# Moving ScalarE's copies of x ahead of its other copies, and GpSimd's last rows into the expert stage, in a sketch-attention and hash-routing kernel on one Trainium2 core

## The chip, the cores and the metric

One core of one Trainium2 chip runs the kernel. The metric is the device time of one execution in microseconds (us). The kernel before takes 200.77 us, the median of 3 runs (200.69 to 201.09). The profiled execution took 200.42 us and its records span 198.7 us. All times inside the profile are counted from the start of that span.

The engines are TensorE (PE in the profile; PEld is its loading of weights), VectorE (DVE), ScalarE (ACT), GpSimd (POOL) and SyncE (SP, which here only starts transfers).

## What is computed

Two blocks follow each other. The first is an attention without softmax: q and k are turned into 64 features each by products of two 8-wide sketches, keys and values are summed into one 64 x 32 matrix per head, and each query reads that matrix and divides by a normaliser. The second block sends each of the 4352 rows to one of 8 experts, chosen by a hash of its token number, and applies two layers with a ReLU between.

```python
# batch 4, heads 4, seq 1088, head_dim 32, r 8; experts 8, width 128, hidden 1024
def phi(x):
    a = einsum('rd,bhsd->bhsr', S1, x)
    b = einsum('rd,bhsd->bhsr', S2, x)
    return einsum('bhsi,bhsj->bhsij', a, b).reshape(..., r * r)
kv  = einsum('bhsf,bhsd->bhfd', phi(k), v);  z = phi(k).sum(over s)
x   = einsum('bhsf,bhfd->bhsd', phi(q), kv) / (einsum('bhsf,bhf->bhs', phi(q), z) + 1e-6)
x   = x.transpose(0, 2, 1, 3).reshape(4352, 128)
e   = token_ids * 2654435761 % 8
out[rows of e] = relu(x[rows of e] @ w1[e]) @ w2[e]
```

## The kernel before

The kernel fixes the order of the instructions on each engine itself: within one engine they run as the program text emits them. So the place of a copy in the text is its place in the engine's queue.

Each batch has 1088 positions: 1024 "main" ones in two groups of 512 (`g = 0, 1`), and a "tail" of 64. The attention of one batch makes these steps. TensorE multiplies features of k by v (`kv_products`), ScalarE spreads the result over block-diagonal matrices `m` in 16 small copies (`kv_diagonal`) and two for the tail (`kv_tail`), and TensorE multiplies the features of q by `m` (`x_products`, two tiles in a group, each followed by a copy from PSUM by ScalarE).

```python
ps   = tile_pool(name="ps", bufs=4, space=PSUM)     # k, q products, transposes, hp
ps_x = tile_pool(name="ps_x", bufs=2, space=PSUM)   # x products
ps_o = tile_pool(name="ps_o", bufs=2, space=PSUM)

def x_products(b, g, fT, m, psum=x_bank):           # x_bank: a tile of ps_x
    for h0 in range(0, H, 2):                       # two tiles in a group
        p = psum([P, 2, Q * DA], "x_ps")
        for h in range(2):
            for fb in range(FB):
                nc.tensor.matmul(p[:, h], fT[...], m[fb][...], ...)
        nc.scalar.copy(xes[b % 2][...], p[:])       # line 617

def transposed(src, g):                             # 4 transposes of k, then ScalarE's copy
    p = bank([P, H, P], "kT_ps")
    ...
    nc.scalar.copy(kT[:], p[:])                     # line 426
```

`copied(ab_ps)` copies the sketch products of k or of q from PSUM (two copies, line 467), `route_tiles_p()` is one scaling pass of ScalarE over a routing table (line 393), and `q_tail_copied` copies the tail's products of q. The loop over the first two batches (`EB` is 2) is where they meet:

```python
for b in range(EB):
    kv = kv_products(b, ...)
    if b > 0: abk_ps = k_products(kTs)
    abq_ps = q_products(qT, T)
    va = values(v_t[b + 1], T, work, "")
    ...
    m = kv_diagonal(b, kv)
    if b > 0:
        abk = copied(abk_ps)
        route_tiles_p()
    if b == 0:
        tail = q_tail_copied(abt_ps)
    abq = copied(abq_ps)
    m_tail = kv_tail(b, kv)
    if b == 0:
        kTs = [transposed(k_t[b + 2], g) for g in range(0, T, Q)]
    kp = k_features(abk, T, work, "")               # VectorE
    ...
    for g in range(GQ):
        x_products(b, g, fTs[g], m)
    x_tail_products(b, m_tail)
    qT = q_blocks(q_t[b + 2], T)
    if b == 0: ... route_rows(0); route_tiles()     # VectorE
    else:
        kTs = [transposed(k_t[b + 2], g) for g in range(0, T, Q)]
        route_rows(1)
    denominators(b, ...)                            # VectorE
    for g in range(GQ): x_main(b, g, nc.gpsimd)     # rows of x, then their transfer to memory
    x_tail(b, nc.gpsimd)
    ...
```

The last two batches follow outside the loop. The rows of x go to a scratch tensor in memory (`x_rows`). The expert stage gathers them by index, 128 rows at a time, with an indirect transfer that GpSimd starts (`fetch_tile`), turns them on their side (`turn_in`, a transfer; `join_in`, VectorE), and multiplies. The first 16 gathered tiles take rows of batches 0 and 1 alone; only the later ones, of the second round over the experts, read rows of batches 2 and 3.

```python
denominators(e, 0, GQ * HQ + H)                     # e: the last batch
for g in range(GQ):
    x_main(e, g, nc.gpsimd)
x_tail(e, nc.gpsimd)
...
def at(g, c, f, *a): ...                            # f is emitted beside step c of expert group g
ahead = [(k, j) for k in range(3, 11) for j in range(tiles_of(k)[1])]
for g, n in enumerate((2, 4, 2, 2, 2, 2, 2, 2)):
    for c in range(n): at(g, 1 + c, fetch_tile, *ahead.pop(0))
for k in range(2, G):
    at(k - 1, 0, turn_in, k)
    at(k - 1, 5, join_in, k)
for g in range(G - 1):                              # 16 groups of 8 steps
    for c in range(FC):
        layer1(g, c)                                # 2 matmul records, then hT by ACT or DVE
        if g > 0: layer2(g - 1, c)                  # 2 matmul records
        for f in beside.get((g, c), ()): f()
```

Each `fetch_tile` of these first copies its indices on VectorE into one of four small buffers, so that VectorE waits in its queue for the gather of four tiles earlier.

Of the kernel before, what the change touches and what calls it, by code (L numbers as in the profile page):

```python
# [30 lines left out]
def kernel(  # L31
# [12 lines left out]
    nc = tc.nc  # L44
    P = 128
    B, H, S, D = q.shape
# [4 lines left out]
    T = S // P  # L51
    SM = T * P
    SP = S - SM
    TT = B // 2
    Q = P // D
# [28 lines left out]
    def bank(shape, name):  # L84
        return ps.tile(shape, F32, tag="b", name=name)
# [13 lines left out]
    def tail_rows(b):  # L99
        return slice(b // TT * SP, (b // TT + 1) * SP)  # L100

    def load_tail_part(t, src, b, eng):
        eng.dma_start(t[tail_rows(b)].rearrange("p t h d -> p (t h) d"),
                      src[b:b + TT, :, SM:, :].rearrange("t h p d -> p (t h) d"))

    def load_tail(src, name, n=B):

        t = const.tile([P, TT, H, D], F32, name=name)
        for b in range(0, n, TT):
            load_tail_part(t, src, b, nc.sync)  # L110
        return t

    def load_main(src, b, tag):
# [11 lines left out]
    k_t, v_t, q_t = [], [], []  # L125
# [23 lines left out]
    k_tail = load_tail(k, "k_tail")  # L149
    v_tail = load_tail(v, "v_tail")  # L150
    q_t.append(load_main(q, 1, "q"))
    q_tail = load_tail(q, "q_tail", TT)
    v_t.append(load_main(v, 1, "v"))
    for b in range(2, B):
        load_batch(b)
# [53 lines left out]
    GQ = T // Q  # L209
# [12 lines left out]
    hi, lo = s64[:, :, 1], s64[:, :, 0]  # L222
# [169 lines left out]
    def route_tiles_p():  # L392
        nc.scalar.activation(tiles[:, :, 0], in_tile[:], AF.Copy, scale=p1[:])
# [23 lines left out]

    x_dram = nc.dram_tensor("x_rows", (N, DM), F32)

    def transposed(src, g):  # L420

        p = bank([P, H, P], "kT_ps")
        for h in range(H):
            nc.tensor.transpose(p[:, h], src[:, h, g:g + Q].rearrange("p t d -> p (t d)"), ident[:])
        kT = work.tile([P, H, P], F32, tag="kT", name="kT", bufs=2)
        nc.scalar.copy(kT[:], p[:])
        return kT
# [35 lines left out]
    def ab_tile():  # L463
        return work.tile([P, T, H, 2, R], F32, tag="ab", name="ab", bufs=3)
# [5 lines left out]
    def copied(ab_ps):  # L470

        ab = ab_tile()
        for g in range(0, T, Q):
            copy_ab(ab, ab_ps, g)
        return ab
# [59 lines left out]
    def kv_tail(b, kv):  # L535

        m = m_tails[b % 2]
        for h in range(2):
            r = slice(h * R * R, (h + 1) * R * R)
            nc.scalar.copy(m[r, :, h], kv[r, :, h * DA:(h + 1) * DA])  # L540
        return m
# [15 lines left out]
    def q_features(ab, g):  # L557

        f = work.tile([P, Q, H, FB * D], F32, tag="f", name="f", bufs=1)
        features(f[:].rearrange("p q h (i j) -> p (q h) i j", i=R), ab[:, g * Q:(g + 1) * Q].rearrange("p q h x r -> p (q h) x r"))  # L560
        fT = feats.tile([P, H * FB, P], F32, tag="fT", name="fT", bufs=3)
        nc.vector.transpose(fT[:].rearrange("p k (q s) -> p k q s", q=Q), f[:].rearrange("p q h (k d) -> p (h k) q d", d=D))  # L562
        return fT
# [44 lines left out]
    def x_products(b, g, fT, m, psum=x_bank):  # L608

        for h0 in range(0, H, 2):  # L610
# [3 lines that stand above are left out]
                    nc.tensor.matmul(p[:, h], fT[:, (h0 + h) * FB + fb],  # L614
                                     m[fb][:, h0 + h].rearrange("p t d -> p (t d)"),
                                     start=(fb == 0), stop=(fb == FB - 1), skip_group_check=True)
            nc.scalar.copy(xes[b % 2][:, (g * H + h0) * Q:(g * H + h0 + 2) * Q].rearrange("p (h t) d -> p h (t d)", h=2), p[:])  # L617
# [12 lines left out]
    dens, rows_of = {}, {}  # L630
# [5 lines left out]
        nc.vector.tensor_scalar(den, xes[b % 2][:, lo:hi, D], 1e-6, None, op0=OP.add)  # L636
        nc.vector.reciprocal(den, den)  # L637

    def x_main(b, g, eng):
        if g == 0:  # L640
            rows_of[b] = work.tile([P, T, H, D], F32, tag="xs", name="xs", bufs=1)
        eng.tensor_tensor(rows_of[b][:, g * Q:(g + 1) * Q].rearrange("p t h d -> p h t d"),  # L642
                          xes[b % 2][:, g * HQ:(g + 1) * HQ, 0:D].rearrange("p (h t) d -> p h t d", h=H),
                          dens[b][:, g * HQ:(g + 1) * HQ].rearrange("p (h t) -> p h t", h=H).unsqueeze(3)
                          .to_broadcast([P, H, Q, D]), op=OP.mult)
        n = parts(b)
        if n > 1 or g == GQ - 1:
            ts = slice(g * Q, (g + 1) * Q) if n > 1 else slice(0, T)
            lo = b * S + ts.start * P
            nc.sync.dma_start(x_dram[lo:lo + SM // n].rearrange("(p t) d -> p t d", t=T // n),  # L650
                              rows_of[b][:, ts].rearrange("p t h d -> p t (h d)"))

    def x_tail(b, eng):
        rows = tail_rows(b)
        xs_tail = work.tile([P, H, D], F32, tag="xs_tail", name="xs_tail", bufs=1)
        eng.tensor_tensor(xs_tail[rows], xes[b % 2][rows, GQ * HQ:, 0:D],
                          dens[b][rows, GQ * HQ:].unsqueeze(2).to_broadcast([SP, H, D]), op=OP.mult)
        nc.sync.dma_start(x_dram[b * S + SM:(b + 1) * S], xs_tail[rows].rearrange("p h d -> p (h d)"))


    route_experts()
    kTs = [transposed(k_t[0], 0)]
# [3 lines left out]
    route_scan()  # L666
    va = values(v_t[0], T, work, "", None)
    route_firsts()
    load_tail_part(q_tail, q, TT, nc.gpsimd)
    abk = ab_tile()  # L670
    kp = work.tile([P, T, H, R, R], F32, tag="kp", name="kp", bufs=1)
    parts_ps = [k_products(kTs[g:g + 1]) for g in range(GQ)]
# [5 lines left out]
    for g in range(GQ):  # L678
        ts = slice(g * Q, (g + 1) * Q)
        nc.scalar.copy(va[:, ts, :, 0:D], v_t[0][:, :, ts].rearrange("p h t d -> p t h d"))  # L680
    kTs = [transposed(k_t[1], g) for g in range(0, T, Q)]
    kv = kv_products(0, (kp, va), (kp_tail, va_tails), None, upto=Q)
# [6 lines left out]
    abq = ab_tile()  # L689
# [5 lines left out]
    for u, va_tail in enumerate(va_tails):  # L695
        rows = tail_rows(u * TT)
        nc.gpsimd.tensor_copy(va_tail[rows, :, :, 0:D], v_tail[rows])
    kv = kv_products(0, (kp, va), (kp_tail, va_tails), kv, Q + 2)
    route_digits(digits)
    abt = k_tail_products(kTt)  # L700
    abk_ps = k_products(kTs)
    kv = kv_products(0, (kp, va), (kp_tail, va_tails), kv, T)
    abk = copied(abk_ps)
    fTs = [q_features(abq, 0)]
# [5 lines left out]
    for b in range(EB):  # L710
        kv = kv_products(b, (kp, va), (kp_tail, va_tails), None if b else kv)
        if b > 0:
            abk_ps = k_products(kTs)
# [3 lines that stand above are left out]
            route_slots()  # L717
        if b == 0:
            abt_ps = q_tail_products(qT_tail)
        m = kv_diagonal(b, kv)  # L720
        if b > 0:
            abk = copied(abk_ps)
            route_tiles_p()
        if b == 0:
            tail = q_tail_copied(abt_ps)
        abq = copied(abq_ps)
        m_tail = kv_tail(b, kv)
        if b == 0:
            kTs = [transposed(k_t[b + 2], g) for g in range(0, T, Q)]
        kp = k_features(abk, T, work, "")  # L730
        if b == 0:
            fT_tail = q_tail_features(tail)
        for g in range(GQ):
            x_products(b, g, fTs[g], m)
        x_tail_products(b, m_tail)
        qT = q_blocks(q_t[b + 2], T)
        if b == 0:
            fTs = [q_features(abq, 0)]
            route_rows(0)
            route_tiles()  # L740
        else:
            kTs = [transposed(k_t[b + 2], g) for g in range(0, T, Q)]
            route_rows(1)
        denominators(b, 0, GQ * HQ + H)
        for g in range(GQ):
            x_main(b, g, nc.gpsimd)
        x_tail(b, nc.gpsimd)
        if b == 0:
            load_experts(range(E // 2, E - 2))
        if b == 0:  # L750
            fTs.append(q_features(abq, 1))
        else:
            fTs = [q_features(abq, 0)]
# [83 lines left out]
    b, e = EB, EB + 1  # L837
    kv = kv_products(b, (kp, va), (kp_tail, va_tails))
    idx = route_list()
    abk_ps = k_products(kTs)  # L840
    abq_ps = q_products(qT, T)
    va = values(v_t[e], T, work, "")
    fTs.append(q_features(abq, 1))
    m = kv_diagonal(b, kv)
    abk, abq = copied(abk_ps), copied(abq_ps)
    m_tail = kv_tail(b, kv)
# [7 lines left out]
    kv = kv_products(e, (kp, va), (kp_tail, va_tails))  # L854
# [5 lines left out]
    m_tail = kv_tail(e, kv)  # L860
    load_experts([E - 1], nc.scalar)
    fTs = [fT, q_features(abq, 1)]
# [8 lines left out]
    x_products(e, 1, fTs[1], last_m)  # L871
    x_tail_products(e, m_tail)
    denominators(e, 0, GQ * HQ + H)
    for g in range(GQ):
        x_main(e, g, nc.gpsimd)
    x_tail(e, nc.gpsimd)

    feats.release()
    hots.release()
# [125 lines left out]
    def at(g, c, f, *a):  # L1005
        beside.setdefault((g, c), []).append(lambda: f(*a))
# [8 lines left out]
    for g, n in enumerate((2, 4, 2, 2, 2, 2, 2, 2)):  # L1015
        for c in range(n):
            at(g, 1 + c, fetch_tile, *ahead.pop(0))
    assert not ahead
    for k in range(11, G):
        for j in range(tiles_of(k)[1]):  # L1020
            at(k - 3, 1 + j, fetch_tile, k, j)
# [28 lines left out]
    g, lo = G - 1, GL - P  # L1050
# [40 lines left out]
    with tc.For_i(0, turns):  # L1091
# [19 lines left out]
        at = moe.tile([P, C], F32, tag="at", name="at", bufs=1)  # L1111
# [3 lines left out]
        rows = moe.tile([P, C, P], BF16, tag="hT", name="rows", bufs=2)  # L1115
# [66 lines left out]
```

## Time and profile before

| Engine | busy us | share of the span |
|---|---|---|
| PE | 187.1 | 94% |
| PEld | 156.0 | 79% |
| DVE | 108.2 | 54% |
| POOL | 104.9 | 53% |
| ACT | 73.5 | 37% |

The shares are averages over two stages of different nature. From the start to about 65 us (the attention and the routing) all engines take turns; from 65 us to about 190 us (the experts) TensorE runs nearly alone. A share for the whole span does not say what a change in one of them brings. What is to be read is where TensorE stands idle, since everything at the end hangs on its last product.

In the timelines each line has the start in us, the busy time in us of the merged instructions, the engine, the line of the kernel, the operation, what it writes and reads, and how many instructions were merged. A bracket at the end gives the idle time of that engine ahead of the instruction and what ended it. The busy times of TensorE's records overlap each other a little, so starts are compared with starts.

### The profile page before, as it was taken

To read this page: it belongs to the slowest core of one execution; us is meant where nothing else is said; L and a number is where in the kernel's file an instruction comes from. 1 tells how busy PE (TensorE), PEld (TensorE's weight loads), DVE (VectorE), ACT (ScalarE), POOL (GpSimd) and SP (SyncE) were. 2 spreads that over 40 slices of the span, in tenths; PEclk is the share of its full clock that TensorE was granted. 3 is DMA by queue.
4 is the path that set the end of the run, shared out by engine and by line. 5 is a ranking of instruction groups with operands and counts; after the bars stand their busy time and mean duration, and the time that the engine had idled before them with its cause. 6 is when DMAs were issued, how large, how long until landed. Compare 5 with 4: busy or idle time off the path is not lost. (4 is left out here: it accounts for less than half of the span.)

```text
span 198.7 us, 3355 instructions
## 1 busy us (share of the span) xinstructions
PE 187.1 (94%) x1066; PEld 156.0 (79%) x1066; DVE 108.2 (54%) x299; ACT 73.5 (37%) x227; POOL 104.9 (53%) x141
## 2 busy tenths in 40 slices
PE   8999969799999999999999999999999999999970
PEld 3889969799998888788888887777777777677960
DVE  5699999589659634434443553544537454332320
ACT  6543953944637412323323332313323131322120
POOL 7328963327642677276468466556365540534541
PEclk9999999999999999999999999999999999999995
DMA  4999999995186453143143244234251331410100
GB/s 135 298 189 296 352 353 337 348 361 190 26 241 196 154 165 92 43 92 79 41 107 84 54 91 105 56 78 69 52 113 42 92 75 33 78 26 25 47 23 14
DMA packets 40242, 26.10 MB, mean 131 GB/s; under 512 B 21273, under 2 KB 37404, under 8 KB 40224
## 3 DMA queue, kind: packets, MB, share of 16 engines
q1 hardware_dynamic: 35360, 19.08, 35.3%
q0 software_dynamic: 2336, 4.66, 8.9%
q10 hardware_dynamic: 2528, 2.13, 3.6%
q8 instruction: 9, 0.15, 0.3%
q14 instruction: 9, 0.07, 0.1%
HBM read 17.47 MB, written 4.59 MB: 111 GB/s over the span
## 5 line engine op out<-in xcount | busy, mean ns | idle before, releaser
L892 PE MATMUL hp<-xT,w 128*128 128x256 f32 (+3 forms) x272 | 81.9, 394 | 0.4 <-DVE hT L765 0.4
L900 PE MATMUL op<-hT,w 128*128 128x256 f32 (+2 forms) x256 | 79.0, 399 | 0.0
L765 DVE TENSOR_SCALAR hT<-hp 128x256 f32<-128x256 f32 (+3 forms) x68 | 29.7, 439 | 64.6 <-PE hp L892 39.7
L903 POOL DMA_INDIRECT out_dram<-os,put x36 | 36.3, 1010 | 45.7 <-DVE os L956 31.1
L892 PEld LDWEIGHTS hp<-xT,w 128*128 128x128 f32 x272 | 49.7, 190 | 12.9 <-issue 1.0
L900 PEld LDWEIGHTS op<-hT,w 128*128 128x128 f32 x256 | 48.1, 190 | 12.9
L763 ACT ACTIVATE hT<-hp 128x256 f32<-128x256 f32 (+3 forms) x68 | 27.0, 400 | 68.1 <-PE hp L892 51.1
L757 POOL DMA_INDIRECT xg<-x_rows,idx x34 | 35.3, 1038 | 19.6 <-issue 6.7
L614 PE MATMUL x_ps<-m,fT 128*128 128x132 f32 x128 | 16.2, 280 | 3.0 <-ACT xe L617 3.0
L614 PEld LDWEIGHTS x_ps<-m,fT 128*128 128x128 f32 x128 | 15.0, 190 | 3.7 <-ACT xe L617 3.6
L510 PE MATMUL kv<-va,kp 128*128 128x132 f32 x128 | 15.6, 278 | 0.1
L510 PEld LDWEIGHTS kv<-va,kp 128*128 128x128 f32 x128 | 14.9, 190 | 0.4 <-issue 0.3
L642 POOL TENSOR_TENSOR xs<-xe,den 128x512 f32<-128x512 f32 x6 | 7.3, 1229 | 12.3 <-DVE den L637 10.9
L935 ACT COPY half<-op 128x256 uint16<-128x256 uint16 (+1 forms) x26 | 8.8, 392 | 12.8 <-PE op L900 11.9
L532 ACT COPY m<-kv 32x66 f32<-32x66 f32 x48 | 9.9, 206 | 8.7 <-PE kv L510 8.1
L479 DVE TENSOR_TENSOR kp<-ab 128x1024 f32<-128x1024 f32 x8 | 9.5, 1224 | 4.8 <-ACT ab L467 4.8
L562 DVE STREAM_TRANSPOSE fT<-f 128x1024 f32<-128x1024 f32 x8 | 10.0, 1245 | 0.5
L479 DVE TENSOR_TENSOR f<-ab 128x1024 f32<-128x1024 f32 x8 | 10.0, 1251 | 0.1
L834 DVE COPY xT<-xh_turned 128x256 uint16<-128x256 uint16 (+1 forms) x28 | 8.1, 342 | 0.0
L452 PE MATMUL abq_ps<-s_k,qT 128*128 128x128 f32 (+1 forms) x64 | 7.8, 274 | 0.4 <-DVE qT L687 0.4
L828 DVE COPY xh<-xg 128x256 uint16<-128x256 uint16 (+1 forms) x28 | 7.9, 324 | 0.0
L452 PEld LDWEIGHTS abq_ps<-s_k,qT 128*128 128x128 f32 x64 | 7.5, 192 | 0.5 <-issue 0.5
(172 smaller groups left out, 154.1 us busy)
## 6 DMA issues: line engine op xcount, KB each, us to landing
w<-in_moe_w_dram SPq DMA_DIRECT2D x12, 512.0 KB
w<-in_moe_w_dram ACTq DMA_DIRECT2D x4, 512.0 KB
k<-in_k_dram SPq DMA_DIRECT2D x3, 512.0 KB
q<-in_q_dram SPq DMA_DIRECT2D x3, 512.0 KB
v<-in_v_dram SPq DMA_DIRECT2D x3, 512.0 KB
x_rows<-xs SPq DMA_DIRECT2D x3, 512.0 KB
out_dram<-os,put POOLq DMA_INDIRECT x36
xg<-x_rows,idx POOLq DMA_INDIRECT x34
```

The costliest lines, as they stand in the source:

```text
L452: nc.tensor.matmul(dst, stationary, s.rearrange("p t x r -> p t (x r)").unsqueeze(1).to_broadcast([s.shape[0], n, s.shape[1], 2 * R]), sta ...
L479: eng.tensor_tensor(dst, ab[:, :, 0].unsqueeze(3).to_broadcast(shape), ab[:, :, 1].unsqueeze(2).to_broadcast(shape), op=OP.mult)
L510: nc.tensor.matmul(kv[:].rearrange("p x y -> p (x y)")[:, pr * HA:(pr + 1) * HA], kp[:, t, 2 * pr:2 * pr + 2].rearrange("p h i j -> p (h i ...
L532: copy(m[f][t * D:(t + 1) * D, h::2, t], src)
L562: nc.vector.transpose(fT[:].rearrange("p k (q s) -> p k q s", q=Q), f[:].rearrange("p q h (k d) -> p (h k) q d", d=D))
L614: nc.tensor.matmul(p[:, h], fT[:, (h0 + h) * FB + fb], m[fb][:, h0 + h].rearrange("p t d -> p (t d)"), start=(fb == 0), stop=(fb == FB - 1 ...
L757: nc.gpsimd.indirect_dma_start(out=dst, out_offset=None, in_=x_dram[0:rows], in_offset=bass.IndirectOffsetOnAxis(ap=idx, axis=0), bounds_c ...
L763: nc.scalar.activation(dst, src, AF.Relu if relu else AF.Copy)
L765: return nc.vector.tensor_scalar(dst, src, 0.0, None, op0=OP.max).ins
L892: nc.tensor.matmul(hp[:, 0:hi - lo], w1[:, g % E, c * P:(c + 1) * P], x_columns(first_of(g) + lo, first_of(g) + hi), start=True, stop=True)
L900: nc.tensor.matmul(ops[g][:, 0:hi - lo], w2[:, g % E, c], hTs[g][:, c, lo:hi], start=(c == 0), stop=(c == FC - 1))
L903: st_ = nc.gpsimd.indirect_dma_start(out=out[:], out_offset=bass.IndirectOffsetOnAxis(ap=idx, axis=0), in_=src, in_offset=None, bounds_che ...
```

## The change

It has three parts. In the loop over the first two batches, ScalarE's copies are put in another order: the two copies of x of group 0 come ahead of the copies of q's products; the copies of the transposed k (batch 0) and the scaling pass of the routing table (batch 1) come behind all copies of x. TensorE's order stays as it was: for batch 0 the transposes of k are still emitted ahead of the x products, only their copies are later. Second, the rows of the last batch are computed by GpSimd beside steps 6 and 7 of expert group 1 instead of ahead of the expert stage, and their two transfers are started by GpSimd instead of SyncE. Third, the second half of the tail of q is loaded by SyncE, right behind the first half, instead of by GpSimd.

The first part is for the two banks of x products in PSUM, which TensorE can only write again once ScalarE has emptied them. The second lets GpSimd start the gathers of the expert stage before it turns to rows that are needed later.

```diff
-    q_tail = load_tail(q, "q_tail", TT)
+    q_tail = load_tail(q, "q_tail")
@@
-    def transposed(src, g):
+    def turned(src, g):
         p = bank([P, H, P], "kT_ps")
         for h in range(H):
             nc.tensor.transpose(p[:, h], ...)
+        return p
+    def transposed(src, g):
+        return kT_copied(turned(src, g))
+    def kT_copied(p):
         kT = work.tile([P, H, P], F32, tag="kT", name="kT", bufs=2)
         nc.scalar.copy(kT[:], p[:])
         return kT
@@   x_main and x_tail take the queue of their transfer (dma=nc.sync)
@@
-    load_tail_part(q_tail, q, TT, nc.gpsimd)
@@
         m = kv_diagonal(b, kv)
-        if b > 0:
-            abk = copied(abk_ps)
-            route_tiles_p()
         if b == 0:
             tail = q_tail_copied(abt_ps)
-        abq = copied(abq_ps)
-        m_tail = kv_tail(b, kv)
-        if b == 0:
-            kTs = [transposed(k_t[b + 2], g) for g in range(0, T, Q)]
+            kT_ps = [turned(k_t[b + 2], g) for g in range(0, T, Q)]
+        else:
+            abk = copied(abk_ps)
         kp = k_features(abk, T, work, "")
         if b == 0:
             fT_tail = q_tail_features(tail)
-        for g in range(GQ):
-            x_products(b, g, fTs[g], m)
+        x_products(b, 0, fTs[0], m)
+        abq = copied(abq_ps)
+        m_tail = kv_tail(b, kv)
+        x_products(b, 1, fTs[1], m)
         x_tail_products(b, m_tail)
         qT = q_blocks(q_t[b + 2], T)
         if b == 0:
+            kTs = [kT_copied(p) for p in kT_ps]
             fTs = [q_features(abq, 0)]
             ...
         else:
+            route_tiles_p()
             kTs = [transposed(k_t[b + 2], g) for g in range(0, T, Q)]
@@
     denominators(e, 0, GQ * HQ + H)
-    for g in range(GQ):
-        x_main(e, g, nc.gpsimd)
-    x_tail(e, nc.gpsimd)
@@
+    for g in range(GQ):
+        at(1, 6, x_main, e, g, nc.gpsimd, nc.gpsimd)
+    at(1, 7, x_tail, e, nc.gpsimd, nc.gpsimd)
```

More of the change, by code (lines that the diff above doesn't have):

```diff
@@ L100, in tail_rows, with load_tail @@
         return slice(b // TT * SP, (b // TT + 1) * SP)
[L102 to L106, printed above, removed]
+    def load_tail(src, name):
         t = const.tile([P, TT, H, D], F32, name=name)
-        for b in range(0, n, TT):
-            load_tail_part(t, src, b, nc.sync)
+        for b in range(0, B, TT):
+            nc.sync.dma_start(t[tail_rows(b)].rearrange("p t h d -> p (t h) d"),
+                              src[b:b + TT, :, SM:, :].rearrange("t h p d -> p (t h) d"))
         return t
@@ L637, in denominators, with x_main @@
         nc.vector.reciprocal(den, den)
-    def x_main(b, g, eng):
+    def x_main(b, g, eng, dma=nc.sync):
         if g == 0:
@@ L649, in x_main, with x_tail @@
             lo = b * S + ts.start * P
-            nc.sync.dma_start(x_dram[lo:lo + SM // n].rearrange("(p t) d -> p t d", t=T // n),
-                              rows_of[b][:, ts].rearrange("p t h d -> p t (h d)"))
-    def x_tail(b, eng):
+            dma.dma_start(x_dram[lo:lo + SM // n].rearrange("(p t) d -> p t d", t=T // n),
+                          rows_of[b][:, ts].rearrange("p t h d -> p t (h d)"))
+    def x_tail(b, eng, dma=nc.sync):
         rows = tail_rows(b)
@@ L657, in x_tail @@
                           dens[b][rows, GQ * HQ:].unsqueeze(2).to_broadcast([SP, H, D]), op=OP.mult)
-        nc.sync.dma_start(x_dram[b * S + SM:(b + 1) * S], xs_tail[rows].rearrange("p h d -> p (h d)"))
+        dma.dma_start(x_dram[b * S + SM:(b + 1) * S], xs_tail[rows].rearrange("p h d -> p (h d)"))
     route_experts()
```

## The prediction, made before the changed kernel was run

> **What bounds the kernel now.** I read the page's busy shares first: TensorE 94%, the others 37 to 54%. Then the table of stages, to see where the missing 6% are. TensorE's idle time is 6.6 us after 190 us (the last rows leaving), and before that only 0.96 us in 0 to 10, 0.49 in 10 to 20, 0.29 in 20 to 25, 1.38 in 25 to 30, 1.33 in 35 to 40, 0.13 in 60 to 80, 0.37 in 80 to 85 and 0.39 in 180 to 190. Everything else is TensorE at work, so a change that leaves its work alone can win these gaps and no more. Then the timeline of TensorE, to see who ends the two large ones:
>
> ```profile
> 22.75 1.97 PE L614 MATMUL x_ps<-m,fT 128*128 128x132 f32 x16
> 26.38 2.07 PE L614 MATMUL x_ps<-m,fT 128*128 128x132 f32 x16 [1.67 <-ACT xe L617]
> ...
> 36.43 2.02 PE L614 MATMUL x_ps<-m,fT 128*128 128x132 f32 x16
> 39.78 2.07 PE L614 MATMUL x_ps<-m,fT 128*128 128x132 f32 x16 [1.33 <-ACT xe L617]
> ```
>
> Each line of 16 is one group of x, two tiles. The reader sees the second group stand behind a ScalarE copy of x, 1.67 us in batch 0 and 1.33 us in batch 1. ScalarE's timeline says why:
>
> ```profile
> 19.44 3.49 ACT L532 COPY m<-kv 32x66 f32<-32x66 f32 x16 [0.76 <-PE kv L510]
> 22.96 0.85 ACT L590 COPY ab_tail<-abq_ps 32x64 f32<-32x64 f32 x4
> 23.82 0.27 ACT L591 COPY ab_tail<-abq_ps 128x128 f32<-128x128 f32 x1
> 23.98 0.66 ACT L467 COPY ab<-abq_ps 128x256 f32<-128x256 f32 x2
> 24.51 0.44 ACT L540 COPY m_tail<-kv 64x66 f32<-64x66 f32 x2
> 24.97 1.07 ACT L426 COPY kT<-kT_ps 128x512 f32<-128x512 f32 x2
> 25.93 0.68 ACT L617 COPY xe<-x_ps 128x264 f32<-128x264 f32 x2
> ...
> 36.63 0.65 ACT L467 COPY ab<-ab_ps 128x256 f32<-128x256 f32 x2
> 37.16 1.33 ACT L393 ACTIVATE tiles<-in_tile,p 128x1224 bf16<-128x1224 bf16 x1
> 38.38 0.64 ACT L467 COPY ab<-abq_ps 128x256 f32<-128x256 f32 x2
> 38.89 0.43 ACT L540 COPY m_tail<-kv 64x66 f32<-64x66 f32 x2
> 39.35 0.66 ACT L617 COPY xe<-x_ps 128x264 f32<-128x264 f32 x2
> ```
>
> The first x tile of batch 0 is ready about 1 us after 22.75, but its copy starts at 25.93, because three other sets of copies are in the queue before it. In batch 1 the first tile is ready at about 37.4 and its copy starts at 39.35. There are two banks for x, both full, so TensorE stops. ScalarE is not overloaded (37% busy); its order is wrong.
>
> In the expert stage I compared the starts of TensorE's pairs, 0.43 us apart when nothing waits. Two places are off: from 75.23 to 75.84 (0.18 us lost) and from 81.63 to 82.59 (0.53 lost, 0.10 in the pair before). For the first, the timelines of VectorE and of GpSimd:
>
> ```profile
> 73.29 0.15 DVE L809 COPY idx<-get 128x1 int32<-128x1 int32 x1 [0.90 <-DMA xg<-x_rows,idx]
> 74.66 0.15 DVE L809 COPY idx<-get 128x1 int32<-128x1 int32 x1 [1.21 <-DMA xg<-x_rows,idx]
> ```
>
> ```profile
> 67.56 2.05 POOL L642 TENSOR_TENSOR xs<-xe,den 128x512 f32<-128x512 f32 x2 [1.38 <-DVE hT L765]
> 69.69 0.53 POOL L656 TENSOR_TENSOR xs_tail<-xe,den 64x128 f32<-64x128 f32 x1
> 70.49 1.04 POOL L757 DMA_INDIRECT xg<-x_rows,idx  x1 [0.27 <-POOL xs_tail L656]
> ```
>
> Here VectorE stands 0.90 and 1.21 us behind gathers, and GpSimd started these late because it made the last batch's rows first (67.56 to 70.2). VectorE's join of the next input columns (75.06) is late by that, and TensorE's 75.84 waits for it.
>
> **What the Trainium skill says.** "PSUM — Partial Sum Buffer", The four PSUM rules: a matmul's output lies in one bank, and PSUM is TensorE's only way out. So a tile of 264 floats takes a bank and must be copied before the bank is used again; the trace agrees with the 1.67 us above. Its Specifications say that GpSimd reaches no PSUM, so it could not take over copies of x. "ScalarE: Activation LUTs", What ACT_TABLE_LOAD costs, gives an ACTIVATE 186 ns plus 0.833 ns per element, and 93 ns more for a pointer operand. Estimates from it: 406 ns for 264 elements, 1.30 us for the scaling pass of 1224. The trace has 380 ns and 1.33 us; I use those. "SBUF — State Buffer", SBUF: two separate sides: GpSimd and VectorE can lock each other out of a shared port when VectorE reads two SBUF inputs. Moving GpSimd's rows into the experts could meet that; but VectorE's evictions there read PSUM, and they took 0.42 us beside the rows (67.35 to 70.2) as elsewhere. "DMA: Bandwidth & Descriptors", Issuing engines are not separate DMA queues: all transfers share 16 engines whoever starts them, so the two changed queues move no bytes faster. No run shows that apart yet.
>
> **Batch 0.** No instruction is added on ScalarE, TensorE or VectorE; the sum of work stays. ScalarE is free at 24.09 (end of the 0.27). The first x tile, 8 of 16 matmuls in 1.97 us, is ready at about 23.75, so its copy runs 24.1 to 24.5. TensorE finishes the second tile at about 24.7 and finds the first bank free. The second copy runs to 25.15, before the next bank is asked for (about 25.6). The gap of 1.67 closes. Then q's products (0.66), the tail matrix (0.44) and the first copy of group 1 end at about 26.65; the tail product wants that bank at 26.6, a wait of at most 0.1. The batch's x ends near 27.1 instead of 28.76: **1.6 us won**. The k copies (1.07) follow, done at 28.5; TensorE needs them after the next kv product (3.87 + 0.61), at 31.3. VectorE wants q's copies at 26.6 and has them at 25.8.
>
> **Batch 1.** TensorE comes to x at 34.8, m is complete at about 35.0 (all shifted by 1.6, the same touch as before). Copies of k's products to 35.65, first x copy to 36.3, second after its tile (36.7) to 37.1; group 1 starts at 36.7 without a gap. q's copies and the tail matrix end at 38.25, the next x copy at 38.6, the tail product wants its bank at 38.65. So 1.33 more, and the sum of both batches is about **3.0 us**, the 1.67 + 1.33 of the rows above. The scaling pass (1.33) now ends near 40.7 and the k copies near 41.8; TensorE wants the first with the routing product at 47.15 - 3.0 = 44.1 and the second at 45.2. VectorE gets k's copy 1.6 us earlier (it waited 2.31 us for it at 37.03), ends kp at 37.7 and so is ahead of the kv product that now starts at 40.1. GpSimd's rows of batch 1 move up with it, if their buffer is free of the transfer of batch 0; I put that at about 41.
>
> **Batches 2 and 3** keep their order; each step there waits for a product of TensorE or a copy of it, so it moves up by 3.0 as a block. Gathers start at about 48 instead of 50.55 and are wanted at 59.
>
> **Experts.** GpSimd starts the gathers of chunk 3 at about 63.6, where before shifted by 3.0 it would be 67.5. Both VectorE waits (0.90, 1.21) go and with them TensorE's 0.18. The rows (2.05 + 0.53) and two started transfers (an estimate of 1 us each, from the 0.95 us that the tail's load took on GpSimd) then lie at about 72.5 to 77, ahead of gathers that are wanted two groups later (14 us), and the rows themselves are read only from group 4 on, near 90. The loss at 81.63 is not explained: ScalarE and VectorE both stood still with products ready. It may go or stay; I count 0.15 of its 0.63.
>
> **q's tail.** One transfer of 64 KB goes from GpSimd (0.95 us of its queue at 6.24, where it waits for data till 12.99 anyway) to SyncE, 0.6 us there. VectorE reads it at 18.4. I count zero.
>
> **The sum:** 1.6 + 1.4 + 0.18 + 0.15 = 3.3 us. 200.77 - 3.3 = 197.5; I say **197.4 us**.
>
> **Rivals.** (1) *A new wait takes the place of the old:* VectorE is without a gap from 25 to 34.7 and does not move up in batch 0, so TensorE running ahead could meet VectorE's features of q for group 1 (ready 34.72, wanted at 36.7) or row table (ready 40.2, wanted 44.1). The slack is 2 us, so I doubt it; it would leave 1.7 of 3.0 us, about 199. (2) *The gain is given back at the experts* by weights or gathers not there yet: the transfers run full until 46 us, and only GpSimd's gathers could be late; they have 10 us. About 200 if so. (3) *GpSimd's rows in group 1 hold back gathers or evictions*: 0.5 us or so lost, about 198. (4) *The unexplained standstill goes altogether*: 196.9.
>
> **Range and chances.** The 3.0 is read from two gaps and has nothing to hide behind, since TensorE is in one chain from there to the end. The rest is 0 to 0.8 us up, or 0.5 to 1 us down. Range 196.5 to 198.6. Faster by over 2% needs less than 196.75, a win of 4.0 us: 0.12. Within 2%: 0.87. Slower: 0.01.
>
> **What would show it.** TensorE's timeline after: second groups of x at 24.7 and 36.7 without a bracket of over 0.2 us; the first pair of the experts at about 62 instead of 64.97; no wait of VectorE's index copies in group 1; the span near 195.4. I am wrong if the brackets are gone but the first expert pair comes later than 62.5 (rival 1), or comes at 62 and the span is above 196 (rivals 2, 3).

## The result and the profile after

The changed kernel takes 197.79 us, the median of 4 runs (197.51 to 197.99), against 200.88 us of the kernel before (4 runs beside it, 200.69 to 201.09). The ratio is 0.9845, with a 95% interval of 0.9828 to 0.9862: 1.5% less. The span of the profile went from 198.7 to 196.2 us. The engines' busy times and shares of the changed kernel, from its page:

```profile
PE 186.0 (95%) x1066; PEld 155.8 (79%) x1066; DVE 112.2 (57%) x299; ACT 74.0 (38%) x227; POOL 105.5 (54%) x142
```

The counts of instructions are those of before but for the one transfer more that GpSimd starts (two of the rows, one of q's tail less), yet VectorE is busy 4.0 us longer (108.2 before). Nothing was added to VectorE, so something made its instructions longer. That is the second half of this story.

The timeline of TensorE in the changed kernel: the x products of batches 0 and 1, the way into the experts, and one place in the experts.

```profile
22.39 3.77 PE L617 MATMUL x_ps<-m,fT 128*128 128x132 f32 x32
26.09 0.45 PE L626 MATMUL x_ps<-m_tail,fT_tail 128*64 128x66 f32 x4
...
34.14 3.82 PE L617 MATMUL x_ps<-m,fT 128*128 128x132 f32 x32
37.90 0.45 PE L626 MATMUL x_ps<-m_tail,fT_tail 128*64 128x66 f32 x4
...
58.39 0.44 PE L823 MATMUL xp<-ident,xg 128*128 128x128 f32 x2 [0.18 <-ACT xe L620]
59.08 2.04 PE L617 MATMUL x_ps<-m,fT 128*128 128x132 f32 x16 [0.25 <-DVE den L639]
...
61.42 1.99 PE L892 MATMUL hp<-xT,w 128*128 128x256 f32 x8
...
78.58 0.59 PE L900 MATMUL op<-hT,w 128*128 128x256 f32 x2
80.15 0.67 PE L892 MATMUL hp<-xT,w 128*128 128x256 f32 x2 [0.98 <-ACT half L935]
80.66 0.59 PE L900 MATMUL op<-hT,w 128*128 128x256 f32 x2
```

Where the kernel before had two lines of 16 with a bracket, there is now one line of 32 in each batch: nothing stopped TensorE between the two groups, so the view merged them. The two short waits at 58.39 and 59.08 are new. At 80.15 an expert's first product comes 1.57 us after the pair ahead of it instead of 0.43 us: 1.14 us lost. The first expert pair starts at 61.42 (before 64.97), the last matmul group at 187.62 (before 190.45).

ScalarE's timeline of the same kernel shows the new order at work:

```profile
23.48 0.27 ACT L594 COPY ab_tail<-abq_ps 128x128 f32<-128x128 f32 x1
23.64 0.38 ACT L620 COPY xe<-x_ps 128x264 f32<-128x264 f32 x1
24.39 0.38 ACT L620 COPY xe<-x_ps 128x264 f32<-128x264 f32 x1 [0.37 <-PE x_ps L617]
24.67 0.65 ACT L470 COPY ab<-abq_ps 128x256 f32<-128x256 f32 x2
25.20 0.44 ACT L543 COPY m_tail<-kv 64x66 f32<-64x66 f32 x2
25.66 0.38 ACT L620 COPY xe<-x_ps 128x264 f32<-128x264 f32 x1
...
26.74 1.06 ACT L429 COPY kT<-kT_ps 128x512 f32<-128x512 f32 x2
```

The first copy of x starts at 23.64, 1.25 us after its product began (before 25.93, 3.18 us after), and now ScalarE is the one that waits (0.37) for TensorE.

VectorE's features of k in batch 1 in the kernel before:

```profile
37.03 2.36 DVE L479 TENSOR_TENSOR kp<-ab 128x1024 f32<-128x1024 f32 x2 [2.31 <-ACT ab L467]
```

VectorE's timeline of the changed kernel, the same features and then the experts:

```profile
34.76 3.64 DVE L482 TENSOR_TENSOR kp<-ab 128x1024 f32<-128x1024 f32 x2 [0.38 <-ACT ab L470]
...
67.04 0.21 DVE L812 COPY idx<-get 128x1 int32<-128x1 int32 x2
...
68.76 0.20 DVE L812 COPY idx<-get 128x1 int32<-128x1 int32 x2
...
72.22 3.06 DVE L831 COPY xh<-xg 128x256 uint16<-128x256 uint16 x2
...
79.38 0.67 DVE L837 COPY xT<-xh_turned 128x256 uint16<-128x256 uint16 x2 [1.90 <-DMA xh_turned<-xh]
```

GpSimd's in the experts, then SyncE's start of the transfer that turns chunk 3:

```profile
63.40 1.00 POOL L760 DMA_INDIRECT xg<-x_rows,idx  x1 [0.77 <-DVE idx L812]
...
71.83 1.00 POOL L760 DMA_INDIRECT xg<-x_rows,idx  x1 [0.30 <-issue]
72.85 2.06 POOL L645 TENSOR_TENSOR xs<-xe,den 128x512 f32<-128x512 f32 x2
75.21 0.64 POOL L653 DMA_DIRECT2D x_rows<-xs  x1 [0.30 <-POOL xs L645]
75.92 0.39 POOL L659 TENSOR_TENSOR xs_tail<-xe,den 64x128 f32<-64x128 f32 x1
```

```profile
75.30 1.19 SPq L832 DMA_TRANSPOSE xh_turned<-xh  x1
```

The features of k in batch 1 take 3.64 us instead of 2.36, which is 1.3 of the 4.0 us. GpSimd now makes rows and values of its own beside them: in every kernel below that has part 1 the second of the two products lies on GpSimd's copy of v and takes 2.46 us, and in those without part 1 it meets no work of GpSimd and takes 1.22. In the experts the index copies no longer wait. But the two half copies that prepare chunk 3 for its turning (`xh`, from memory tile to memory tile within the chip) take 3.06 us, where an undisturbed pair takes 0.48 us: 2.6 of the 4.0 us. They end at 75.28, shortly after GpSimd's rows (72.85 to 74.9). The view of that one tile splits the pair: of 28 such copies the median is 288 ns, and one alone took 2853.

```profile
L831 DVE COPY xh<-xg x28: 274/288/2853, 65.7 to 166.3; 128x256 uint16<-128x256 uint16 x20, 128x384 uint16<-128x384 uint16 x8
```

From there the chain to TensorE is short. The transfer that turns the chunk is issued at 75.30, VectorE's join waits 1.90 us for it and starts at 79.38, and TensorE's 80.15 needs its columns: the join ends at 80.05. The bracket at 80.15 names ScalarE's `half` copies instead, which had ended at 79.86. Those copies belong to every group, and they stop nothing where the join is early (in the kernel with the reduction below it starts at 77.49).

To add up the experts I compared the starts of TensorE's pairs of 256 columns, 0.43 us apart when nothing waits, in every kernel. Before: 0.26 behind the late gathers and 0.74 at the standstill near 82, together 1.0 us. After: 1.22 here and 0.43 near 101, together 1.65 us. So TensorE came to the experts 3.55 us earlier, and the experts gave 0.65 us back.

### The profile page after: what moved, and what is told of

It reads as the page before. It is cut to its first block, busy times and chain, and to the rows that moved or that the text cites. A ratio compares the mean times of both kernels' runs of the same rounds, so it can differ in the third digit from the quotient of the medians.

```text
span 196.2 us, 3350 instructions
## 1 busy us (share of the span) xinstructions
PE 186.0 (95%) x1066; PEld 155.8 (79%) x1066; DVE 112.2 (57%) x299; ACT 74.0 (38%) x227; POOL 105.5 (54%) x142
## 5 line engine op out<-in xcount | busy, mean ns | idle before, releaser
L903 POOL DMA_INDIRECT out_dram<-os,put x36 | 36.8, 1022 | 43.2 <-DVE os L956 27.2
L760 POOL DMA_INDIRECT xg<-x_rows,idx x34 | 34.7, 1019 | 19.0 <-issue 7.9
L617 PE MATMUL x_ps<-m,fT 128*128 128x132 f32 x128 | 15.7, 278 | 0.2 <-DVE den L639 0.2
L482 DVE TENSOR_TENSOR kp<-ab 128x1024 f32<-128x1024 f32 x8 | 10.7, 1382 | 1.0 <-ACT ab L470 1.0
L831 DVE COPY xh<-xg 128x256 uint16<-128x256 uint16 (+1 forms) x28 | 10.5, 417 | 0.0
L956 DVE COPY os<-turned 128x256 uint16<-128x256 uint16 (+1 forms) x26 | 7.4, 319 | 3.8 <-issue 2.5
```

What stands on the lines that cost most here:

```text
L482: eng.tensor_tensor(dst, ab[:, :, 0].unsqueeze(3).to_broadcast(shape), ab[:, :, 1].unsqueeze(2).to_broadcast(shape), op=OP.mult)
L617: nc.tensor.matmul(p[:, h], fT[:, (h0 + h) * FB + fb], m[fb][:, h0 + h].rearrange("p t d -> p (t d)"), start=(fb == 0), stop=(fb == FB - 1 ...
L760: nc.gpsimd.indirect_dma_start(out=dst, out_offset=None, in_=x_dram[0:rows], in_offset=bass.IndirectOffsetOnAxis(ap=idx, axis=0), bounds_c ...
L831: nc.vector.tensor_copy(xh[:, x * w:(x + 1) * w], _half(xg3[k][:].rearrange("p a b -> p (a b)")[:, 0:w], x))
L903: st_ = nc.gpsimd.indirect_dma_start(out=out[:], out_offset=bass.IndirectOffsetOnAxis(ap=idx, axis=0), in_=src, in_offset=None, bounds_che ...
```

## The experiments

The main theory was that part 1 (the order on ScalarE) brings all of the gain, and that part 2 (the rows beside the experts) costs some, because GpSimd's rows shut VectorE's half copies out of memory. The rivals were that part 2 or part 3 also matters, and that the half copy waits for something else in its queue. All ratios are to the kernel before, run beside it on the same chip. They are not quotients of the two medians, since they leave out the executions at a lowered clock, one of which is the only profile of the last kernel.

| Kernel | median us (before) | ratio, 95% interval | x of batch 0 to first expert pair, us | lost by TensorE in the experts, us |
|---|---|---|---|---|
| before | | 1 | 42.22 | 0.99 |
| changed | 197.79 (200.88) | 0.9845, 0.9828 to 0.9862 | 39.03 | 1.64 |
| changed, again | 197.35 (200.56) | 0.9827, 0.9802 to 0.9852 | 38.90 | 1.53 |
| part 1 alone | 196.72 (200.03) | 0.9843, 0.9820 to 0.9866 | 38.86 | 1.09 |
| part 2 alone | 200.67 (200.03) | 1.0037, 1.0022 to 1.0053 | 42.21 | 1.21 |
| part 3 alone | 200.27 (200.03) | 1.0014, 0.9999 to 1.0029 | 41.93 | 0.94 |
| parts 1 and 3 | 197.58 (199.91) | 0.9871, 0.9847 to 0.9895 | 38.98 | 1.72 |
| chunk 3's halves on ScalarE | 196.39 (200.03) | 0.9813, 0.9785 to 0.9840 | 38.83 | 0.66 |
| all halves on ScalarE | 197.00 (200.56) | 0.9809, 0.9781 to 0.9837 | 39.22 | 0.74 |
| chunk 3's halves as a reduction | 195.94 (199.91) | 0.9795, 0.9771 to 0.9818 | 38.89 | 0.00 |
| rows in group 2 | 199.67 (200.56) | 0.9936, 0.9911 to 0.9960 | 39.23 | 3.50 |
| rows in group 2, without part 3 | 199.21 (200.56) | 0.9920, 0.9889 to 0.9951 | | |

The last two columns are read from one profile each: the start of the first x product subtracted from that of the first expert pair, and the sum of the late pairs. The first leaves out the start-up, which differs by 0.9 us from profile to profile, with part 3 and without (the first x product starts between 21.80 and 22.75).

**Part 1 alone.** The order of the loop as in the changed kernel, rows and tail as before.

```diff
-    q_tail = load_tail(q, "q_tail")
+    q_tail = load_tail(q, "q_tail", TT)          # second half by GpSimd again
@@
+    for g in range(GQ): x_main(e, g, nc.gpsimd)  # ahead of the experts again
+    x_tail(e, nc.gpsimd)
@@
-    for g in range(GQ):
-        at(1, 6, x_main, e, g, nc.gpsimd, nc.gpsimd)
-    at(1, 7, x_tail, e, nc.gpsimd, nc.gpsimd)
```

> The kernel before with part 1 alone (ScalarE's order). My theory: the two brackets of 1.67 and 1.33 us ahead of the second groups of x are the whole gain, so 3.0 us less than before, about 197.8 us; GpSimd's last rows still stand ahead of the gathers of chunk 3, so VectorE's index copies wait about 1 us each again. Rival (the gain of 3.55 us up to the experts came in part from the other parts): only 2.5 us or less.

It gives 0.9843, 3.3 us less than before, which can't be told from the whole change and isn't the rival's 2.5. Its attention is as short (38.86 us). In the experts it has the late gathers of the kernel before, somewhat worse (0.58 us), and a wait of 0.52 us at 79.27.

**Part 2 alone.** The kernel before with `x_main` and `x_tail` of the last batch moved to group 1, their transfers started by GpSimd.

> The kernel before with part 2 alone (rows of the last batch beside the experts). Theory of the port: GpSimd's rows run just when VectorE splits the halves of chunk 3, block it for 2 us or more, and TensorE waits about 1.1 us at the start of group 3; against it stand 0.2 to 0.3 us of waits for gathers that go, and perhaps the standstill of 0.7 us: 0 to 1 us slower than before. Rival (rows moved out of the way of gathers help): 0.3 to 1 us faster.

It is slower than the kernel before by 0.37%, a small difference that the interval separates from none. VectorE's and GpSimd's timelines of this kernel:

```profile
74.84 3.05 DVE L828 COPY xh<-xg 128x256 uint16<-128x256 uint16 x2
...
82.03 0.63 DVE L834 COPY xT<-xh_turned 128x256 uint16<-128x256 uint16 x2 [1.93 <-DMA xh_turned<-xh]
```

```profile
75.47 2.06 POOL L642 TENSOR_TENSOR xs<-xe,den 128x512 f32<-128x512 f32 x2
```

The long pair, its 3.05 us and the join's wait of 1.93 us are all there without parts 1 and 3, so they belong to part 2.

**Part 3 alone.** Both halves of q's tail loaded by SyncE.

> The kernel before with part 3 alone (second half of q's tail by SyncE). Expected: nothing, within 0.3 us. Rival: the 0.36 us that the changed kernel was ahead already at 18 us comes from this part; then 0.3 to 0.4 us faster, and the first kv products start that much earlier.

It makes no difference that its interval can separate from none. The standstill near 82 us stands as it was.

**Chunk 3's half copies on ScalarE.** One line of the changed kernel:

```diff
-            nc.vector.tensor_copy(xh[...], _half(...))
+            (nc.scalar.copy if k == 3 else nc.vector.tensor_copy)(xh[...], _half(...))
```

> The changed kernel, but the two half copies of chunk 3 (ahead of its transposing transfer) run on ScalarE instead of VectorE. Theory of the port: GpSimd's rows do not hold ScalarE up, the copies take 0.4 us each and not 3.06 us together, the transfer starts about 2 us earlier, TensorE's 1.14 us at the start of group 3 go: about 196.6 us. Rival (the transfer of the rows, 512 KB, that GpSimd starts at 75.2 holds the transposing transfer up): the wait for the transfer stays and the time is about 197.8 us.

ScalarE's and GpSimd's timelines:

```profile
72.80 0.71 ACT L831 COPY xh<-xg 128x256 uint16<-128x256 uint16 x2
```

```profile
72.51 2.06 POOL L645 TENSOR_TENSOR xs<-xe,den 128x512 f32<-128x512 f32 x2
```

The same data are copied while GpSimd's rows run from 72.51, and take 0.71 us. So neither the data nor a semaphore held the copies back. The join starts at 76.93 without a wait and the 1.14 us are gone. The 0.66 us that TensorE still loses lie elsewhere, at 81.69: an eviction by VectorE stood in its queue behind a copy of outputs that waited 1.92 us for its transfer. The time is 0.9813, about 0.6 us better than the changed kernel where 1.2 were expected, and its interval overlaps that of the changed kernel.

**The changed kernel again, and all half copies on ScalarE.** The first is unchanged; the second moves the copies of all 14 chunks.

> The changed kernel once more, beside the next ones on one chip: about 3.1 us faster than before, with VectorE's two half copies of chunk 3 taking about 3 us and TensorE losing about 1.1 us at the start of group 3.

> The changed kernel with the half copies of all chunks on ScalarE (28 copies of about 0.4 us, ScalarE has room). Theory of the port: as with chunk 3 alone, 0.6 to 1.2 us faster than the changed kernel; VectorE has more room too, so the later losses near 101 us may go. Rival (ScalarE becomes late with its half of the hT tiles): as slow as the changed kernel.

The repeat shows the long copy again (2774 ns) and 1.53 us lost. With all copies on ScalarE the time, 0.9809, is that of moving chunk 3's alone, so nothing is seen to come from the other pairs. It is 0.35 us less than that of the repeat beside it, not the 0.6 to 1.2 expected, and the intervals overlap.

**Chunk 3's halves as a reduction on VectorE.** Same engine, same place in the queue, same data; a maximum over an axis of length 1 in place of the copy.

```diff
-                nc.vector.tensor_copy(xh[...], src)
+                nc.vector.tensor_reduce(xh[...], src.unsqueeze(2), axis=AX.X, op=OP.max)   # k == 3
```

> The changed kernel with one thing replaced: chunk 3's two half copies stay on VectorE and at the same place in its queue, beside GpSimd's rows, but each is written as a reduction (maximum) over an axis of length 1 instead of a copy. Main theory: the copy waits because its form takes both of VectorE's paths into SBUF, one of which GpSimd holds while it makes the rows; the Trainium skill, "SBUF — State Buffer" (the engine ports' consequences), says that a reduction has no such form on this chip and never meets GpSimd. Then each of the two takes 0.3 to 0.4 us (256 elements, estimate from the 0.42 us of an eviction of 256), the pair ends by about 73, the transposing transfer is issued by 73.5 instead of 75.3, TensorE's 1.14 us at the start of group 3 is gone, and the time is that of the kernel with ScalarE's copies, 0.980 to 0.983. Rival: any work of VectorE from SBUF to SBUF is held back beside GpSimd's rows, or the copy waits for something else in the queue; then the pair again takes about 3 us, TensorE loses 1.1 again, and the ratio is 0.983 to 0.986.

VectorE's timeline, then GpSimd's:

```profile
72.31 0.73 DVE L833 TENSOR_REDUCE xh<-xg 128x256 uint16<-128x256 uint16 x2
...
77.49 0.50 DVE L841 COPY xT<-xh_turned 128x256 uint16<-128x256 uint16 x2
```

```profile
72.04 1.00 POOL L760 DMA_INDIRECT xg<-x_rows,idx  x1 [0.30 <-issue]
73.07 2.06 POOL L645 TENSOR_TENSOR xs<-xe,den 128x512 f32<-128x512 f32 x2
```

Each of the two takes 0.41 us, where an undisturbed copy takes 0.28, and nothing holds them: the transfer is issued at 73.07, the join doesn't wait, and TensorE loses nothing at all in the experts (this profile is also free of the standstill described below). This is the fastest kernel run, 0.9795 (0.9771 to 0.9818). Its interval lies below that of the changed kernel's first comparison and overlaps that of the repeat. One reserve stands: the pair ends at 73.04, just as the records put the start of the rows (73.07). The comparison is with the long copy of the changed kernel, the first of its pair, alone in this view:

```profile
72.22 2.85 DVE L831 COPY xh<-xg 128x256 uint16<-128x256 uint16 x1
```

It started 0.63 us ahead of the recorded start of the rows, would have ended at 72.5, and was held to 75.07. In the repeat the second of the pair was the long one; it started 0.56 us ahead. So the copy is kept out some time before the rows' own record begins, and the second reduction, from 0.43 us ahead to the start of the rows, got through there. What keeps a copy out so early isn't settled. GpSimd issues an indirect transfer just ahead of the rows, and towards its end such an issue can hold a copy on its own. In the kernel with the rows in group 2 (below) no rows follow it, and the second copy, started 0.59 us into the issue, took 0.50 us, to 0.1 us behind the end of the issue:

```profile
72.25 0.50 DVE L831 COPY xh<-xg 128x256 uint16<-128x256 uint16 x1
```

```profile
71.66 1.00 POOL L760 DMA_INDIRECT xg<-x_rows,idx  x1 [0.30 <-issue]
```

So the reduction is shown to pass where copies were held. That it would also pass beside the multiplications themselves is not shown.

**Parts 1 and 3, without part 2.**

> The changed kernel without its second part: the new order of ScalarE's copies and the load of q's tail as in the changed kernel, GpSimd's last rows ahead of the experts as in the kernel before. Main theory: it keeps the 3.2 to 3.5 us of the attention; the half copies of no chunk take over 0.8 us, while VectorE's index copies in group 1 wait again for gathers (1.3 us twice) and TensorE loses 0.4 to 0.6 there in place of the 1.14 of the changed kernel. Ratio 0.981 to 0.986, within 0.3% of the changed kernel: the second part brings nothing in sum. Rival: the second part is worth its 0.2 us as predicted, or the tail's load matters together with the new order; then this one is slower than the changed kernel by 0.2 us or more, 0.986 or above.

It is 0.9871. VectorE waits for gathers again:

```profile
70.28 0.15 DVE L812 COPY idx<-get 128x1 int32<-128x1 int32 x1 [1.48 <-DMA xg<-x_rows,idx]
...
71.57 0.15 DVE L812 COPY idx<-get 128x1 int32<-128x1 int32 x1 [1.14 <-DMA xg<-x_rows,idx]
```

TensorE loses 0.69 us by that and 0.86 at another standstill near 80. This kernel and the one with part 1 alone differ only in part 3, and their intervals overlap. The ratio lies where the rival put it (0.986 or above), but part 1 alone, which lacks part 2 as well, is at 0.9843, and the intervals of all of them overlap that of the changed kernel (0.9827 and 0.9845). What part 2 brings as it stands can't be told from nothing.

One forecast failed and tells more than the ratio. No pair of half copies was to take over 0.8 us, but chunk 2's took 1.28, its first copy beside GpSimd's rows in their old place. VectorE's and GpSimd's timelines:

```profile
65.69 1.08 DVE L831 COPY xh<-xg 128x256 uint16<-128x256 uint16 x1
```

```profile
64.58 2.05 POOL L645 TENSOR_TENSOR xs<-xe,den 128x512 f32<-128x512 f32 x2 [2.04 <-ACT hT L766]
```

The copy ends 0.14 us behind the rows. Seven profiles have a half copy of VectorE that meets these two multiplications: chunk 2's before, with part 3 alone, with part 1 alone and here, chunk 3's in the changed kernel, in its repeat and with part 2 alone. They took 0.46, 0.35, 0.75, 1.08, 2.85, 2.77 and 2.85 us, according to when they began, and each ended 0.14 to 0.16 us behind the second multiplication. So the kernel before had these holds too, at a place where TensorE lost nothing by them.

**Rows in group 2.** The rows placed behind the first scatter of group 2, where no half copy of chunk 3 is near; once with and once without part 3.

```diff
-        at(1, 6, x_main, e, g, nc.gpsimd, nc.gpsimd)
-    at(1, 7, x_tail, e, nc.gpsimd, nc.gpsimd)
+        at(2, 6, x_main, e, g, nc.gpsimd, nc.gpsimd)
+    at(2, 6, x_tail, e, nc.gpsimd, nc.gpsimd)
```

> The changed kernel, but GpSimd makes the last rows beside step 6 of group 2, behind the first scatter, where VectorE only empties PSUM. Theory of the port: the half copies of chunk 3 take 0.5 us again and TensorE's 1.1 us at group 3 go: 0.6 to 1.2 us faster than the changed kernel. Rival (the 512 KB transfer of the rows is what delays the transposing transfers): the wait moves to group 4, about as slow as the changed kernel. A third way: the rows come too late for the gathers of group 4 and TensorE waits near group 7: slower.

> As the one before, but q's tail loaded as in the kernel before (second half by GpSimd). If the tail's load costs nothing either way: equal within 0.3 us. If SyncE's load costs the 0.28 us that the single test showed (0 to 0.6): 0.3 us faster.

The half copies of chunk 3 took 0.69 us and group 3 started without loss, as expected. But the time is worse, 0.9936 and 0.9920 (the intervals overlap, so nothing is seen of q's tail), and the profile gives a reason that was not expected. The timelines of VectorE, ScalarE and TensorE in the first of the two:

```profile
101.62 0.76 DVE L768 TENSOR_SCALAR hT<-hp 128x256 f32<-128x256 f32 x2 [5.21 <-remote]
```

```profile
98.09 0.38 ACT L766 ACTIVATE hT<-hp 128x256 f32<-128x256 f32 x1 [4.30 <-PE op L900]
101.71 0.66 ACT L766 ACTIVATE hT<-hp 128x256 f32<-128x256 f32 x2 [3.23 <-remote]
```

```profile
98.53 0.70 PE L892 MATMUL hp<-xT,w 128*128 128x256 f32 x2 [0.53 <-issue]
99.07 0.59 PE L900 MATMUL op<-hT,w 128*128 128x256 f32 x2
102.10 0.70 PE L892 MATMUL hp<-xT,w 128*128 128x256 f32 x2 [2.44 <-DVE hT L768]
```

VectorE and ScalarE both stand still with products ready in PSUM, until all four banks are full and TensorE stops: 3.5 us in all.

This is the standstill of the kernel before in a longer form. There, from VectorE's timeline:

```profile
77.81 0.20 DVE L809 COPY idx<-get 128x1 int32<-128x1 int32 x2
82.11 0.76 DVE L765 TENSOR_SCALAR hT<-hp 128x256 f32<-128x256 f32 x2 [4.09 <-PE hp L892]
```

It is near 82 us before and with part 3 alone, near 101 in the changed kernel, at 79 to 80 with parts 1 and 3 or part 1 alone, at 93 with all halves on ScalarE, and at 98 to 102 here. It is absent with part 2 alone, with chunk 3's halves on ScalarE, with the reduction, and in the repeat of the changed kernel. So it isn't bound to an edit: one and the same kernel has it in one execution and not in another. Where it is, it costs TensorE 0.4 to 3.5 us. The bracket names TensorE or nothing that the trace holds. Its cause stays open, and what a single profile loses by it can't be laid to the change that the kernel tests.

## Why the prediction was right, and which of its steps were not

The prediction was 197.4 us, with 196.5 to 198.6 as its range; 197.79 us came out, within 2% of before. The total hides two errors of opposite sign, so its closeness is in part luck.

**Batches 0 and 1: mechanism right, size too small.** The prediction took the brackets, 1.67 and 1.33 us, as the whole gain ("the sum of both batches is about 3.0 us"). The tail products of both batches and the first expert pair in the kernel before:

```profile
28.38 0.45 PE L623 MATMUL x_ps<-m_tail,fT_tail 128*64 128x66 f32 x4
...
41.78 0.45 PE L623 MATMUL x_ps<-m_tail,fT_tail 128*64 128x66 f32 x4
...
64.97 1.35 PE L892 MATMUL hp<-xT,w 128*128 128x256 f32 x5
```

From the start of x to that of the tail product it was 5.63 us in batch 0 and is 3.70; in batch 1, 5.35 and 3.76. That is 1.93 + 1.59 = 3.52 us, and 0.26 more than the bracket in each batch: the two groups with a stop between them took 3.96 and 4.02 us without the bracket, and take 3.70 and 3.76 without the stop. What the 0.26 consists of was not taken apart. (The prediction's sum has 1.4 for batch 1, where its working has 1.33.) Rival 1, VectorE's features or table as a new wait there, did not come: no bracket stands in either batch. VectorE's features of k ended at 38.4 instead of the predicted 37.7, since GpSimd's work now lay beside them, and the kv product that wants them started at 39.2. With the banks emptied in time TensorE doesn't stop.

**Batches 2 and 3 "as a block": nearly.** The first x product to the first expert pair took 42.22 us and takes 39.03, 3.19 less. Of the 3.52, 0.33 were lost on the way; the two new brackets of 0.18 and 0.25 us at 58.39 and 59.08 are the only ones there. The remaining 0.36 of the first pair's 3.55 us lie in the start-up; with part 3 alone the first x product starts at 22.75 as before, so they are not shown to be the change's. The gathers did not move up to 48 at all: the first starts at 50.59 (before 50.55). It did no harm, since they are wanted at 58.

**Experts, the gathers: right.** Chunk 3's start at 63.40 (predicted 63.6), the waits of 0.90 and 1.21 us are gone, and the 0.18 us of TensorE with them.

**Experts, the rows: the step that failed.** The prediction let the rows cost nothing where they were put: they lie "ahead of gathers that are wanted two groups later", and "VectorE's evictions there read PSUM". Their place was right (predicted 72.5 to 77; they ran from 72.85 to 76.3, their second transfer issued by 77.2), and the evictions were indeed not slowed. But VectorE also has the half copies, which read and write SBUF, and one of these pairs lay at just that place. The kernel before already showed one beside the rows, 0.46 us instead of 0.28, and TensorE doesn't run "nearly alone" there: from 65 to 190 us VectorE was busy 55 us and GpSimd 68. The held pair cost 1.14 us of TensorE and 0.08 in the pair behind. That is rival 3, which named gathers and evictions, and put 0.5 us on it.

The prediction had the relevant section in hand and used half of it. "SBUF — State Buffer", SBUF: two separate sides, gives two conditions under which VectorE needs the port that it shares with GpSimd: two SBUF inputs, or an operation "in a 2-port perf mode". The prediction kept the first only. "SBUF — State Buffer", Who interferes with whom, adds that copies can enter these modes, that a reduction cannot on this chip, and that ScalarE never waits for anyone. The runs agree: 2.85 us for one copy of VectorE, 0.41 us for the reduction at the point where the copy was already held, 0.40 us each for ScalarE's copies beside the rows. That it is the port is the page's account; the runs show which forms are held and which aren't, not the port.

**q's tail: right.** Counted zero; alone it makes 1.0014 (0.9999 to 1.0029).

**The standstill: counted as 0.15 us of gain.** It left 82 us and came back near 101: 0.74 us lost before, 0.43 after, so 0.3 us won in this profile. It comes and goes with the execution, so that is not a gain of the change.

**The sum.** Predicted 3.0 + 0.18 + 0.15 = 3.3. In the two profiles: 3.52 - 0.33 in the attention, + 0.26 by the gathers, - 1.22 by the half copies, + 0.31 by the standstill makes 2.54, and 0.36 of start-up 2.90; the last matmul group starts 2.83 us earlier. The last rows take 8.58 us from there instead of 8.25, so the span shrinks by 2.5 us. The prediction's own test for this was right: a first pair near 62 and a span above 196 was to mean rival 2 or 3, and 61.42 and 196.2 came.

## What to carry to other kernels

When a matmul stops for a PSUM bank, read the queue of the engine that empties it: here the copy engine was busy 37% of the time and only its order was wrong, and a reordering without one instruction less gave 3.2 us of 199. Before work of GpSimd is moved to a place where "it has time", list every VectorE instruction there by where it reads and writes: here evictions from PSUM passed (0.42 us), and so did VectorE's transposes of q's features in SBUF (1.25 us), while the half copies, from SBUF to SBUF, were held until GpSimd's work was over and a product of two SBUF operands took 2.46 us instead of 1.22. A transfer issued behind such a copy carries the delay to the next group. If they must meet, let ScalarE make the copy, or try a form of VectorE that isn't held.

## What the runs showed that was not expected

- A VectorE copy of 256 two-byte elements takes 0.27 to 0.29 us; beside two multiplications of GpSimd that take 2.06 us together it took 2.85, 2.77 in the repeat. It was held through both of them, and from 0.35 us or more before the record of the first began (0.28 in the repeat).
- The reduction over an axis of length 1 took 0.41 us for the same elements: slower than an undisturbed copy by 0.13, and faster in that place by 2.4 us.
- Starting a plain transfer took GpSimd 0.64 and 0.62 us; the prediction's estimate, from another transfer on that engine, was 1 us each.
- VectorE and ScalarE can stand still together for 2 to 5 us with products ready, at a place that changes from kernel to kernel, and in one execution of a kernel but not in another. The kernel with the longest one was 0.9 to 1.1% slower than the changed one. No run here shows why.
